# Attention with beacon keys and a maxout projection: loads as FP32 with casts on chip, and transposes by DMA, in place of casting DMAs and transposes on TensorE

## The chip, the cores and the metric

The kernel runs on one core of a Trainium2 chip (trn2). The metric is the device time of one execution in microseconds (us), so less is better. A change counts as faster or slower when it is beyond 2%. Names of the engines in the profile: PE is TensorE (PEld its weight loads), DVE is VectorE, ACT is ScalarE, POOL is GpSimd and SP is SyncE, which does nothing here but issue DMAs. A casting DMA changes the number type on the way. The DMA crossbar writes a tile transposed; such a transfer is called a turn below. PSUM is the memory that TensorE writes its products to.

## The reference

Eight batches, eight heads, 576 tokens and 16 beacon keys of head size 64. All inputs are FP32 in DRAM.

```python
B, H, S, Nb, D = 8, 8, 576, 16, 64
k_all = concat([beacon_k, k], axis=2); v_all = concat([beacon_v, v], axis=2)
scores = q @ k_all.T / sqrt(D)           # masked causally over k, beacons always visible
x = softmax(scores) @ v_all              # (B, H, S, D) -> (B*S, H*D) = (4608, 512)
h = max(x @ w1, x @ w2, x @ w3)          # w: (512, 768)
out = h @ w_out                          # w_out: (768, 512), out FP32 (4608, 512)
```

## The kernel before

Attention goes by batches, in each by four pairs of heads, in each by six chunks of scores. The projection, called FFN here, is cut into 22 units for every 512 tokens: 18 units of the first product (with the maximum taken on VectorE) and 4 of the second. They are put between the chunks of the next batch's attention, so that TensorE has work while ScalarE computes exponentials.

The loads of q, k, v and the weights are casting DMAs of GpSimd: FP32 is read and BF16 lands. Only the first two pairs come as FP32 by the SP and ACT queues and are cast on chip.

```python
def load_qk(b, hs):                      # the same form for v, w_in, w_out
    q_sb, k_sb, _ = load_tiles(b)        # BF16 tiles
    nc.gpsimd.dma_start(out=q_sb[:, hs, :], in_=q[b, hs].rearrange("h (p r) d -> p h (r d)", r=QR))
    # ... k and beacon_k
```

TensorE turns every pair (12 transposes for q, 16 for k), and VectorE copies the result out of PSUM. `qz` holds each head with zeros in the other head's 64 partitions.

```python
def emit_transposes(p):
    # ...
    q_ps = turn(qs, QP, QR)              # nc.tensor.transpose, 12 times
    k_ps = turn(ks, KP, KR)              # 16 times
    for e in range(2):
        hs = slice(64 * e, 64 * e + 64)
        nc.vector.tensor_copy(qz[p % NQZ][e][hs], q_ps[hs])
    nc.vector.tensor_copy(kT, k_ps.rearrange("d r p -> d p r"))
```

Masks of batches 0 and 1 are products on VectorE, because GpSimd is busy writing descriptors then. Later masks are selects on GpSimd. The output leaves through three buffers and the SP queue:

```python
y = ffn_y.tile([128, d_model], FP32, name="y")      # ffn_y has bufs=3
nc.vector.tensor_copy(y, ps)
nc.sync.dma_start(out[row : ...], y[...])
```

Emission order at the start: q and k of batch 0, v of batch 0, q and k of batch 1, first halves of the input weights, v of batch 1, second halves, w_out. In batch 1 nine FFN units are done, from batch 2 on 22 a batch.

The softmax here doesn't subtract the row's maximum and nothing guards it: scores larger than these inputs give would overflow.

## Time and profile before

| | before |
|---|---|
| median of runs | 336.8 us (336.05 to 337.81) |
| profiled span | 333.6 us |
| TensorE busy | 312.4 us, 94% |
| batch 2 begins (its first score product) | 59.9 us, 9 FFN units done |
| one batch after that | 35.4 us |

By stretches: the columns are the stretch, its length, busy us and instruction counts of each engine, granted TensorE clock, DMA share and GB/s.

```profile
core 0: us, PE busy (x) PEld busy (x) DVE busy (x) ACT busy (x) POOL busy (x), PEclk, DMA share, GB/s
0.00:20.00 20.00, 11.10 (x148) 6.31 (x152) 11.79 (x31) 11.44 (x30) 15.95 (x31) 1.00 1.23 167
...
40.00:60.00 20.00, 16.98 (x269) 9.95 (x268) 13.23 (x35) 13.27 (x40) 7.76 (x10) 1.00 1.27 149
60.00:80.00 20.00, 19.87 (x297) 11.27 (x295) 10.93 (x19) 12.99 (x37) 11.48 (x31) 1.00 0.48 73
...
120.00:320.00 200.00, 199.48 (x2392) 107.37 (x2387) 113.82 (x192) 106.24 (x285) 80.30 (x238) 1.00 0.41 63
```

From 120 to 320 us TensorE is busy 199.48 of 200 us (and 19.87 of 20 at 60 to 80), so only work taken off TensorE can shorten that part. The first 60 us have gaps.

What a pair's transposes cost there, from the timeline of TensorE (start, length, operation):

```profile
162.25 0.31 PE L247 MATMUL sc<-qz_109,kT 128*128 128x336 bf16 x1
162.49 0.45 PE L212 MATMUL sc<-ident,q_sb 96*64 96x96 bf16 x12
...
163.14 1.04 PE L334 MATMUL fps<-xT,w_sb 128*128 128x512 bf16 x4
```

From the start of the transposes at 162.49 us to the next projection matmul at 163.14 us is 0.65 us a pair.

### The profile page before, as it was taken

The page shows a single profiled execution, that of the slowest core. Times are in us where ns is not written, and L with a number is a line of the kernel's source. Part 1 is how long each engine was busy: PE and PEld are TensorE (multiplying, and loading weights), DVE is VectorE, ACT ScalarE, POOL GpSimd, SP SyncE. Part 2 cuts the span into 40 slices and gives each one's busy share as a digit, 9 for nine tenths or more (in the row PEclk, how much of TensorE's full clock was granted, in tenths as well). Part 3 has the DMA queues.
Part 4 walks back from the last instruction along what each step waited for, and adds up shares of the span by engine and source line. Part 5 has one row for each costly group of instructions (what it writes and reads, how often), then busy time and mean ns, then how long its engine had stood idle before and what let it go on. Part 6 is the DMA issues. An engine that isn't in the chain of part 4 may idle for free.

```text
span 333.6 us, 9819 instructions
## 1 busy us (share of the span) xinstructions
PE 312.4 (94%) x4064; PEld 171.4 (51%) x4064; DVE 190.4 (57%) x360; ACT 185.1 (55%) x505; POOL 153.4 (46%) x399
## 2 busy tenths in 40 slices
PE   1888788999999999999999999999999999999994
PEld 1454455555555555655565656555555554444441
DVE  4665467654655655656565565546556545555552
ACT  2798675765675557665765567656755562120210
POOL 8929851266545745474626654665433330000000
PEclk9998999999999999999999999999999999999998
DMA  8999999059702983099408940596002200402204
GB/s 172 151 177 127 165 161 154 9 71 178 98 2 29 175 120 28 2 162 160 26 4 116 194 36 4 78 182 88 2 2 65 66 0 2 127 2 63 62 2 126
DMA packets 62352, 28.24 MB, mean 85 GB/s; under 512 B 42980, under 2 KB 57404, under 8 KB 62308
## 3 DMA queue, kind: packets, MB, share of 16 engines
q0 software_dynamic: 55808, 16.98, 48.0%
q1 hardware_dynamic: 6188, 10.05, 10.5%
q10 hardware_dynamic: 312, 0.59, 0.7%
q8 instruction: 32, 0.52, 0.6%
q14 instruction: 12, 0.10, 0.1%
HBM read 35.13 MB, written 9.44 MB: 134 GB/s over the span
## 4 chain that ended last, share of the span: by engine, by line
PE 81%; DVE 8%; ACT 6%; DMA 2%; issue 1%; SPq 0%; DVEq 0%
PE fps L334 34%; PE fps L351 12%; PE sc L247 12%; PE pv L295 11%; PE sc L334 5%; ACT at_sb L255 5%; PE sc L212 3%; PE sc L351 2%; DMA q_120<-in_q_dram 2%; DVE kT L226 2%; DVE xT L312 2%; DVE hT L344 1%; DVE qz_109 L225 1%; PE fps L212 1%; ACT hT L342 0%
## 5 line engine op out<-in xcount | busy, mean ns | idle before, releaser
L255 ACT ACTIVATE at_sb<-sc 128x288 bf16<-128x288 f32 (+4 forms) x384 | 129.7, 404 | 64.3 <-PE sc L247 61.6
L334 PE MATMUL fps<-xT,w_sb 128*128 128x512 bf16 x564 | 144.2, 380 | 0.8
L273 POOL TENSOR_SCALAR_AFFINE_SELECT at_sb<-at_sb 128x132 bf16<-128x132 bf16 (+2 forms) x288 | 80.9, 300 | 102.6 <-ACT at_sb L255 97.6
L344 DVE TENSOR_TENSOR hT<-hT,fps 128x512 bf16<-128x512 bf16 x94 | 64.4, 686 | 58.1 <-PE fps L334 43.8
L334 PEld LDWEIGHTS <-w_sb 128*128 128x128 bf16 x648 | 59.0, 98 | 56.9 <-issue 2.5
L247 PEld LDWEIGHTS <-kT 128*128 128x128 bf16 (+1 forms) x384 | 37.2, 102 | 44.1 <-issue 4.6
L342 ACT CAST hT<-fps 128x512 bf16<-128x512 f32 x47 | 27.5, 585 | 48.2 <-PE fps L334 45.7
L351 PE MATMUL fps<-w_out_sb,hT 128*128 128x512 bf16 x180 | 44.1, 380 | 0.0
L312 DVE TENSOR_TENSOR xT<-pv,recip 128x288 bf16<-128x288 f32 x64 | 27.7, 454 | 26.1 <-ACT recip L307 19.8
L165 POOL DMA_DIRECT2D v_sb<-in_v_dram x40 | 34.2, 863 | 6.8 <-DMA w_out_sb<-in_moe_w_out_dram 3.7
L295 PE MATMUL pv<-at_sb,v_sb 128*32 128x288 bf16 (+4 forms) x1280 | 32.6, 240 | 0.8 <-DVE xT L312 0.8
L295 PEld LDWEIGHTS <-v_sb 128*32 128x32 bf16 (+1 forms) x1280 | 25.6, 97 | 13.3 <-issue 12.0
L359 DVE COPY y<-fps 128x512 f32<-128x512 f32 x30 | 20.7, 691 | 19.5 <-PE fps L351 16.5
L351 PEld LDWEIGHTS <-hT 128*128 128x128 bf16 x216 | 19.9, 98 | 22.4 <-DVE hT L344 3.1
L247 PE MATMUL sc<-qz_103,kT 128*128 128x288 bf16 (+2 forms) x96 | 28.0, 296 | 2.4 <-DVE kT L226 2.0
L247 PE MATMUL sc<-qz_107,kT 128*128 128x288 bf16 (+2 forms) x96 | 27.0, 283 | 2.2 <-DVE kT L226 1.3
L247 PE MATMUL sc<-qz_105,kT 128*128 128x288 bf16 (+2 forms) x96 | 27.8, 294 | 0.3 <-ACT at_sb L255 0.2
L247 PE MATMUL sc<-qz_109,kT 128*128 128x288 bf16 (+2 forms) x96 | 26.9, 282 | 1.0 <-DVE kT L226 0.6
L226 DVE COPY kT<-sc 128x592 bf16<-128x592 bf16 x28 | 21.7, 774 | 0.9
L334 PE MATMUL sc<-xT,w_sb 128*128 128x512 bf16 x84 | 21.6, 379 | 0.0
L269 DVE TENSOR_TENSOR at_sb<-at_sb,mask 128x264 bf16<-128x264 bf16 (+2 forms) x48 | 11.6, 264 | 15.5 <-ACT at_sb L255 15.2
L212 PEld LDWEIGHTS <-q_sb 96*64 96x64 bf16 x384 | 10.7, 112 | 14.0 <-DVE q_sb L152 7.5
(46 smaller groups left out, 205.5 us busy)
## 6 DMA issues: line engine op xcount, KB each, us to landing
out_dram<-y SPq DMA_DIRECT2D x24, 192.0 KB, 2.9
q_sb<-in_q_dram POOLq DMA_DIRECT2D x7, 576.0 KB, 6.2
k_sb<-in_k_dram POOLq DMA_DIRECT2D x7, 576.0 KB, 9.1
v_sb<-in_v_dram POOLq DMA_DIRECT2D x24, 128.0 KB, 5.2
out_dram<-y SPq DMA_DIRECT2D x24, 128.0 KB, 3.0
w_sb<-in_moe_w_dram POOLq DMA_DIRECT2D x24, 96.0 KB, 4.3
out_dram<-y SPq DMA_DIRECT2D x24, 64.0 KB, 2.8
v_sb<-in_v_dram POOLq DMA_DIRECT2D x8, 112.0 KB, 4.9
```

What stands on the lines that cost most here:

```text
L165: nc.gpsimd.dma_start(out=v_sb[lo : lo + n, t], in_=v[b, :, t0 : t0 + n, :].rearrange("h p d -> p h d"),)
L212: nc.tensor.transpose(ps[64 * e : 64 * e + 64, r, :], src[e][:, r * D : (r + 1) * D], ident[0:n, 0:n],)
L226: nc.vector.tensor_copy(kT, k_ps.rearrange("d r p -> d p r"))
L247: nc.tensor.matmul(ps[0:n, 0 : nr * w].rearrange("k (r p) -> k r p", p=w), kT[:, 128 * t : 128 * t + n], qz[p % NQZ][e][:, r0:r1, p0:QP], ...
L255: nc.scalar.activation(out=at_sb[0:n, t, j0 + e, r0:r1, p0:QP], in_=sc[e][0:n, 0 : nr * w].rearrange("k (r p) -> k r p", p=w), func=AF.Exp ...
L273: nc.gpsimd.affine_select(out=view, in_=view, compare_op=ALU.is_ge, fill=0.0, base=QR * p0 + r0 - k_tok[t], pattern=[[1, nr], [QR, p1 - p0 ...
L295: nc.tensor.matmul(ps[32 * j : 32 * j + 32, :, p0:QP], lhsT, at_sb[0:n, t, j, rs, p0:QP], start=(t == 0), stop=(t == n_kt - 1), tile_posit ...
L312: nc.vector.tensor_mul(xs.rearrange("c (r p) -> c r p", p=QP), ps, state["recip", hf])
L334: nc.tensor.matmul(ps, w_in[i][:, ct, 128 * ft : 128 * (ft + 1)], xT[:, ct, t0 : t0 + TOKB], start=(ct == 0), stop=(ct == n_ct - 1),)
L342: nc.scalar.copy(hT[:, ft, :], ps)
L344: nc.vector.tensor_max(hT[:, ft, :], hT[:, ft, :], ps)
L351: nc.tensor.matmul(ps, hT[:, ft, 128 * tt : 128 * (tt + 1)], w_out_sb[:, ft, :], start=(ft == 0), stop=(ft == n_ft - 1),)
```

## The change

The intent: take the transposes of batches 2 to 7 off the engine that limits the kernel, and free GpSimd from writing descriptors. Every load becomes a plain FP32 DMA of the SP queue into one of six staging tiles. Casts are done on VectorE, ScalarE or GpSimd. From batch 2 on the DMA crossbar turns q and k. `x` becomes a ring of four batches to make room, masks are all done on GpSimd, and batch 1 carries 18 FFN units in place of 9.

```diff
-        nc.gpsimd.dma_start(
-            out=q_sb[:, hs, :], in_=q[b, hs].rearrange("h (p r) d -> p h (r d)", r=QR)
-        )
+    st_pool = ctx.enter_context(tc.tile_pool(name="st", bufs=6))
+    def load_w(i, half):
+        st = new_stage(("w", i, half))               # FP32 staging tile
+        # ...
+            nc.sync.dma_start(out=dst[32 * j : 32 * j + 32], in_=wv[j, :, :, half * FH : (half + 1) * FH])
+    def cast_w(i, half, cast):                       # the same form for pairs, k, q, v, w_out
+        st = stage.pop(("w", i, half))
+        cast(w_in[i][:, :, half * FH : (half + 1) * FH], st[:, 0 : n_ct * FH].rearrange(...))
+    def turn_k(b, g):
+        nc.sync.dma_start_transpose(out=batch_tiles(b)[1][:, g]..., in_=k_src[:, g]...)
+    def turn_q(b, g):
+        nc.sync.dma_start_transpose(out=batch_tiles(b)[0][:, g]..., in_=q_src[:, g]...)
-        if b < 2:                                    # masks on VectorE
-            nc.vector.tensor_mul(view, view, m.to_broadcast([n, 2, nr, p1 - p0]))
-            return
+    at_step(0, 1, C(cast_pair, 2, by_pool, by_pool))
+    at_step(1, 1, C(cast_pair, 3, by_pool, by_pool))
+    at_step(1, 3, C(cast_w, 0, 0, by_dve))           # after pair 1, chunk 3
+    at_step(1, 5, C(cast_w, 1, 0, by_dve))
+    at_step(2, 1, C(cast_w, 2, 0, by_dve))
+    at_step(2, 2, C(cast_pair, 4, by_dve, by_pool))
+    # ...
+    at_step(3, 5, L(nc.gpsimd.memset, q_src, 0.0), L(nc.gpsimd.memset, k_src[...], 0.0))
+    for b in range(3, B):
+        p = (b - 1) * PPB
+        d = 1 if b == 3 else 0
+        at_step(p + d, 3, C(cast_k, b, 1, by_pool), L(turn_k, b, 0), L(turn_k, b, 1))
+        at_step(p + d, 4, C(cast_q, b, 0, by_pool), L(turn_q, b, 0))
+        at_step(p + 2, 2, C(cast_q, b, 1, by_pool), L(turn_q, b, 1))
+        # ... casts of v
```

(Cut: the tile shapes, among them a score tile that is packed without gaps, the plan's other steps, the ring's index.) `C` runs a cast, gives the staging tile back and issues the next loads, so the SP queue gets loads, turns and stores in the order in which the program reaches them.

## The prediction

> **What bounds it now.** The table of busy times by stretches shows TensorE busy for all 20 us of every 20 us from 60 to 320 us at full clock; before that it is busy 11.1, 16.3 and 17.0 of 20. The chain of waits puts 81% of the span on TensorE. VectorE (57%), ScalarE (55%) and GpSimd (46%) have room. In the timeline a batch takes about 35.4 us (kT copies at 58.2, 93.2 and 128.5 us).
>
> **What is removed.** In batches 2 to 7 the 28 TensorE transposes of each of 24 pairs go. In the timeline at 162.49 us they hold TensorE until 163.14, 0.65 us by starts, plus about 0.1 us that the change of operation costs where they follow a score product. 24 x 0.65 to 0.75 = 15.6 to 18 us, all on the critical path after 60 us. With them go VectorE copies of 0.46 + 0.46 + 0.77 us per pair (not critical) and two of four score buffers per pair. GpSimd loses some 75 us of descriptor writing; VectorE the mask products of batches 0 and 1 (11.6 us).
>
> **What is added.** GpSimd casts: from its two mask sizes (264 ns for 57 elements, 330 for 132) I estimate 0.21 us + 0.88 ns per element, so 0.67 us for 512, 0.9 for 768, some 11 us a batch beside 13.5 us of masks, in a period of 33: fits, but a pair with casts needs about 9.6 us in a pair of 8.2, caught up in the next. Crossbar turns move 1.8 MB a batch; the Trainium skill (Advanced Engine Details and Errata, section X-Bar Transpose) says they run about as fast as ordinary DMA, 350 to 400 GB/s (estimate: 5 us a batch; no run yet shows it). The sync queue takes turns, loads and stores in order, with waits on casts; of a batch's four output tiles only the fourth needs a store (the first's), which is issued ahead of the turns. The ring splits 18 FFN units into 256-column halves: about nothing.
>
> **Start.** Loads of FP32 read the same bytes; the first pair should land a little earlier (score at 8.7 us now). But GpSimd then has masks plus 2 us casts plus v casts in batch 0, and casts on VectorE wait in order for loads; I expect the first value product some 3 to 5 us later than 19.8 us, and batch 1 stretched by loads, to about 66 us instead of 59.9. Against that, batch 1 carries 18 FFN units instead of 9, 0.86 us of TensorE each, so 7.8 us less for the tail. Net about 0, give or take 5.
>
> **Sum.** 336.2 - 16.5 + 1.3 = 321 us; range 311 to 333. Chances: faster by over 2% 0.82, within 2% 0.12, slower 0.06.
>
> **What would show it right.** TensorE still busy 20 of 20 from about 70 us; a batch period of 32.6 to 33; transposes only in 8 pairs; VectorE busy down by about 40 us; GpSimd's idle time mostly waits on the exponential; batch 2 beginning at 62 to 70 us with 18 units done.
>
> **What would make it wrong.** The sync queue needing over 33 us a batch for turns (they then arrive late: score products waiting for a DMA); GpSimd casts near twice my estimate (value products waiting for masks); a start that loses more than 10 us to loads queued behind casts; or FFN units stalled by weights cast late.

## More of the kernel before

Bytes "landed" are the bytes that a DMA wrote.

The page of the profile of the kernel before: engine rows in tenths of each of 40 slices of 8.3 us, GB/s landed in each slice, the DMA queues with packets, MB and their time, and the chain that ended last by engine.

```profile
PE   1888788999999999999999999999999999999994
...
DMA  8999999059702983099408940596002200402204
GB/s 172 151 177 127 165 161 154 9 71 178 98 2 29 175 120 28 2 162 160 26 4 116 194 36 4 78 182 88 2 2 65 66 0 2 127 2 63 62 2 126
...
q0 software_dynamic: 55808, 16.98, 48.0%
q1 hardware_dynamic: 6188, 10.05, 10.5%
...
PE 81%; DVE 8%; ACT 6%; DMA 2%; issue 1%; SPq 0%; DVEq 0%
```

From the eighth slice on TensorE is busy without a gap. The DMA row is 8 and then 9 for the first seven slices (to 58 us, with 9.3 MB landed in the first 60 us at a mean of 155 GB/s) and then has pauses. GB/s counts the bytes that land, so for a casting load the bytes read are twice that (the page gives 35.13 MB read, of which the casting queue landed 16.98 MB). TensorE is 81% of the chain.

## The result, and the profile after

The changed kernel ran at 355.99 us (354.31 to 357.76, four runs) beside 336.8 us for the kernel before, ratio 1.057 (95% 1.051 to 1.063). It is slower by 5.7%. A ratio here and below is the mean time of one kernel's fast runs over that of the other's from the same rounds, so it is not quite the ratio of the medians that are quoted.

The page of the changed kernel, the same rows as before (slices of 8.9 us):

```profile
PE   2954655969965799999999999999999999999994
...
DMA  7999999999999999999999999996631300300304
GB/s 192 203 187 202 179 204 173 201 273 150 213 206 253 196 209 219 219 203 189 193 220 195 185 183 239 228 199 140 126 68 31 91 2 0 100 22 20 100 0 120
...
q1 hardware_dynamic: 129200, 55.59, 82.0%
...
PE 67%; DMA 20%; SPq 5%; DVE 3%; POOL 2%; issue 2%; ACT 1%; DVEq 0%; POOLq 0%
```

The DMA row is now 9 from the second slice to the 27th, about 240 us. The one queue that is left carries loads, turns and stores, and the time of its packets is 82.0% of the span. The bytes read are the same in both kernels (35.13 MB on both pages). The chain has 20% DMA, where it had 2%. TensorE has gaps up to the fourteenth slice.

By stretches, as before:

```profile
0.00:20.00 20.00, 11.53 (x110) 6.34 (x110) 8.31 (x16) 11.45 (x29) 9.96 (x30) 1.00 0.98 191
20.00:40.00 20.00, 12.48 (x196) 7.53 (x197) 8.14 (x14) 7.83 (x23) 8.04 (x22) 1.00 1.03 201
40.00:60.00 20.00, 10.11 (x143) 5.19 (x144) 10.14 (x12) 5.72 (x16) 16.07 (x28) 0.58 1.01 179
...
80.00:100.00 20.00, 19.23 (x267) 11.32 (x271) 11.71 (x21) 12.78 (x37) 10.87 (x31) 1.00 1.19 187
100.00:120.00 20.00, 12.06 (x69) 5.53 (x68) 3.69 (x6) 7.65 (x23) 8.71 (x26) 0.83 1.04 223
120.00:320.00 200.00, 195.42 (x2324) 113.99 (x2357) 88.56 (x148) 127.23 (x346) 116.11 (x350) 0.99 0.79 149
```

At 40 to 60 us TensorE is busy for 10.11 of 20 us (16.98 before) at a granted clock of 0.58, and again for only 12.06 at 100 to 120 us. The low clock appears only in stretches where TensorE is partly idle, but not in all of them: at 20 to 40 us it was busy for 12.48 us at 1.00. In the steady part it was 0.99.

Following the batches by the first score product and by the first output tile of each 512 tokens:

| | before | after |
|---|---|---|
| batch 2 begins | 59.9 us, 9 units done | 91.5 us, 18 units done |
| batch 2 (first output tile to the next group's first) | 35.4 us | 45.1 us |
| four batches after that | 141.5 us | 131.1 us |

The first score product of batch 2, before and then after, from the timelines of TensorE:

```profile
59.88 0.29 PE L247 MATMUL sc<-qz_103,kT 128*128 128x288 bf16 x1
```

```profile
91.50 0.65 PE L330 MATMUL sc<-qz,kT 128*128 128x288 bf16 x4
```

A first-product unit takes 0.86 us of TensorE, so nine units more are worth 7.8 us. The start therefore lost 31.6 - 7.8 = 23.8 us, batch 2 lost another 9.7, and the next four batches gave back 10.4, 2.6 us each. That makes 23.1 us; the last batch and the tail gained the rest, down to the 20.9 us between the two profiled spans. **The steady part did what was predicted. The start, and with it batch 2, did not.**

The chain of work up to the beginning of batch 2, by line: first the kernel before to 60 us, then the changed one to 92 us.

```profile
by line: ACT at_sb L255 29.6%; DMA q_120<-in_q_dram 12.4%; PE sc L247 9.6%; PE pv L295 8.9%; PE fps L334 7.8%; PE fps L212 4.1%; DVE kT L226 3.9%; issue 2.9%; ACT hT L342 2.6%; DVE xT L312 2.6%; DVE qz_105 L225 2.3%; DVE qz_103 L225 2.1%; D
```

```profile
by line: DMA st<-in_moe_w_dram 35.8%; DMA st<-in_k_dram 17.0%; DMA st<-in_q_dram 9.9%; PE fps L415 7.5%; SPq L203 6.2%; DMA st<-in_v_dram 5.5%; issue 2.3%; PE sc L330 2.3%; DVE hT L425 2.1%; DVE qz L176 1.8%; DVE xT L392 1.5%; SPq L260 1.2%
```

Before, the chain runs through exponentials (29.6%) and one early load. After, loads of weights, k, q and v are 68% of it. So in the start TensorE waits, by way of other engines, for DMAs. (The chain of this window ends with the SP queue issuing a load, not with batch 2's first product; it leaves TensorE's line of work at 87.3 us.) Its TensorE pieces lie from 62 us on, where a unit took 0.86 us as before, so the low clock of 40 to 60 us isn't on this chain.

Who did the waiting, from the list of waits of the changed kernel (total, times, longest):

```profile
DVE w_sb L280 <- DMA st<-in_moe_w_dram: 20.4, 5, 9.3
...
POOL k_562 L152 <- DMA st<-in_beacon_k_dram: 8.4, 1, 8.4
...
PE fps L415 <- DVE y L440: 6.4, 1, 6.4
```

VectorE waits for weights 20.4 us in all. GpSimd waits 8.4 us for one k. Masks on GpSimd, and copies and maxima on VectorE, stand behind these casts. The last line belongs to batch 2. The timeline of all engines shows it (SPq is the SP queue issuing):

```profile
101.03 1.17 SPq L237 DMA_DIRECT2D st<-in_q_dram  x2
...
102.29 1.04 SPq L448 DMA_DIRECT2D out_dram<-y  x2
...
104.12 7.47 SPq L203 DMA_DIRECT2D st<-in_v_dram  x5
...
109.67 0.69 DVE L440 COPY y<-fps 128x512 f32<-128x512 f32 x1 [9.33 <-DMA out_dram<-y]
```

The fourth output tile needs the first one's buffer. Its store was issued only at 102.29 us, after a batch's k and q loads, though the first tile was ready at 95.2; then its transfer landed among queued loads. VectorE waited 9.33 us, TensorE 6.44.

### The profile page after: what moved, and what is told of

Same layout as the page of the kernel before. It is cut to its first block, busy times and chain, and to the rows that moved or that the text cites. A ratio compares the mean times of both kernels' runs of the same rounds, so it can differ in the third digit from the quotient of the medians.

```text
span 354.5 us, 8835 instructions
## 1 busy us (share of the span) xinstructions
PE 306.2 (86%) x3421; PEld 171.7 (48%) x3464; DVE 157.9 (45%) x259; ACT 187.3 (53%) x505; POOL 182.0 (51%) x520
## 2 busy tenths in 40 slices
DMA packets 129242, 56.16 MB, mean 158 GB/s; under 512 B 113424, under 2 KB 122640, under 8 KB 129200
## 3 DMA queue, kind: packets, MB, share of 16 engines
q1 hardware_dynamic: 129200, 55.59, 82.0%
HBM read 35.13 MB, written 9.44 MB: 126 GB/s over the span
## 4 chain that ended last, share of the span: by engine, by line
PE 67%; DMA 20%; SPq 5%; DVE 3%; POOL 2%; issue 2%; ACT 1%; DVEq 0%; POOLq 0%
PE fps L415 32%; PE fps L432 10%; PE sc L330 10%; DMA st<-in_moe_w_dram 9%; PE pv L373 9%; DMA st<-in_k_dram 4%; PE sc L415 4%; SPq L203 4%; DMA st<-in_q_dram 3%; DMA out_dram<-y 2%; PE sc L432 1%; DMA st<-in_v_dram 1%; POOL k_src L232 1%; POOL at_sb L350 1%; DVE hT L425 1%
## 5 line engine op out<-in xcount | busy, mean ns | idle before, releaser
L338 ACT ACTIVATE at_sb<-sc 128x288 bf16<-128x288 f32 (+4 forms) x384 | 131.1, 404 | 71.9 <-PE sc L330 70.5
L350 POOL TENSOR_SCALAR_AFFINE_SELECT at_sb<-at_sb 128x132 bf16<-128x132 bf16 (+2 forms) x384 | 110.0, 305 | 99.7 <-ACT at_sb L338 93.8
L415 PE MATMUL fps<-xT,w_sb 128*128 128x512 bf16 (+1 forms) x626 | 145.9, 358 | 12.1 <-DVE y L440 6.4
L415 PEld LDWEIGHTS <-w_sb 128*128 128x128 bf16 x720 | 67.6, 98 | 63.4 <-issue 13.5
L330 PE MATMUL sc<-qz,kT 128*128 128x288 bf16 (+4 forms) x384 | 81.6, 302 | 5.3 <-DVE kT L177 3.7
L440 DVE COPY y<-fps 128x512 f32<-128x512 f32 x32 | 22.1, 692 | 32.3 <-PE fps L432 14.6
L373 PEld LDWEIGHTS <-v_sb 128*32 128x32 bf16 (+1 forms) x1280 | 27.3, 101 | 15.8 <-issue 13.2
L373 PE MATMUL pv<-at_sb,ones 128*32 128x288 bf16 (+4 forms) x640 | 22.3, 253 | 14.3 <-DVE xT L392 9.1
L385 ACT ACTIVATE lnd<-pv 128x288 f32<-128x288 f32 x32 | 13.5, 422 | 25.5 <-PE pv L373 24.9
L373 PEld LDWEIGHTS <-ones 128*32 128x32 bf16 (+1 forms) x640 | 15.5, 101 | 21.7 <-issue 20.4
L218 POOL CAST v_sb<-st 128x512 bf16<-128x512 f32 (+1 forms) x40 | 23.4, 614 | 2.4 <-DMA st<-in_v_dram 2.4
L232 POOL CAST k_src<-st 128x256 bf16<-128x256 f32 (+1 forms) x60 | 21.3, 399 | 0.8 <-DMA st<-in_k_dram 0.8
L280 DVE CAST w_sb<-st 128x1536 bf16<-128x1536 f32 x6 | 8.9, 1486 | 20.4 <-DMA st<-in_moe_w_dram 20.4
L248 POOL CAST q_src<-st 96x768 bf16<-96x768 f32 x20 | 15.9, 821 | 0.0
(70 smaller groups left out, 95.2 us busy)
```

The source lines that it names most:

```text
L218: cast(v_sb[0:n, t].rearrange("p h d -> p (h d)"), st[0:n, i * H * D : (i + 1) * H * D],)
L232: cast(k_src[0:n, g, :, t], src[:, g])
L330: nc.tensor.matmul(ps[0:n, 0 : nr * w].rearrange("k (r p) -> k r p", p=w), kT[:, g, j0 // 2, 128 * t : 128 * t + n], qz[:, g, j0 + e, r0:r ...
L338: nc.scalar.activation(out=at_view(at_sb, t, j0 + e, r0, r1), in_=sc[e][0:n, 0 : nr * w], func=AF.Exp, scale=scale,)
L350: nc.gpsimd.affine_select(out=view, in_=view, compare_op=ALU.is_ge, fill=0.0, base=QR * p0 + r0 - k_tok[t], pattern=[[1, nr], [QR, p_max[t ...
L373: nc.tensor.matmul(ps[32 * j : 32 * j + 32, :, p_min[t] : QP], lhsT, at_view(at_sb, t, j, hf * RH, (hf + 1) * RH).rearrange("k (r p) -> k ...
```

## The experiments

Two theories were stated after this reading. RATE: FP32 lands too slowly; what batch 2 needs is 17.7 MB landed (197 GB/s over 90 us; 1.8 MB of it are batch 2's own turns) in place of 9.3 MB. ORDER: engines and queues run in order, and what attention needs stands behind casts, loads and stores that are late. Each run below lists its edit against the changed kernel, unless it says otherwise. Against the kernel before, by the 2% rule, e_hybrid2 is the same and e_half, e_half_w, e_half_mask, e_mask and e_all are unclear; what is read from these is their difference from the changed kernel.

### Kinds of loads by themselves (m_rates)

No attention, wrong output. Each kind of load is issued alone, and VectorE notes the landing.

```diff
+ for kind, dt, issue in [("pair", FP32, by_sp), ("pair", BF16, by_pool), ("w", FP32, by_sp), ...]:
+     for d in phase(kind, dt, issue): landed(d)
```

> A measurement, wrong output on purpose: each kind of load alone, one after the other, FP32 by the sync queue, cast to BF16 by the GpSimd queue, and FP32 (no cast) by the GpSimd queue. Theory RATE (the FP32 loads land too slowly): per byte read, FP32 by the sync queue takes about 1.5 times as long as the cast load (about 195 against 310 GB/s read, from the two traces). If the bytes written are what counts, FP32 by the GpSimd queue is as slow as by the sync queue; if the hardware queue itself is slow, it is as fast as the cast load. Rival ORDER (the rates are alike, and only the order of waits of casts costs): the times of FP32 and cast loads are within 15% of each other. Two queues in turn (sync and ScalarE) should change nothing if the 16 engines are the limit. The four crossbar turns of a batch alone should take 12 to 14 us.

| first issue to last landing, us | FP32 by SP | cast by GpSimd | FP32 by GpSimd |
|---|---|---|---|
| four pairs of q, k | 12.4 | 11.3 | 14.9 |
| three weight halves | 12.4 | 9.9 | 12.7 |
| v of two batches | 13.5 | 12.2 | 14.5 |
| w_out | 6.6 | 7.4 | not run |

The landing of the second and third weight half, FP32 by SP and then cast, from VectorE's timeline:

```profile
50.53 0.15 DVE L102 COPY sink<-f 128x1 f32<-128x1 f32 x1 [3.33 <-DMA f<-in_moe_w_dram]
53.81 0.15 DVE L102 COPY sink<-f 128x1 f32<-128x1 f32 x1 [3.13 <-DMA f<-in_moe_w_dram]
...
62.32 0.15 DVE L102 CAST sink<-b 128x1 f32<-128x1 bf16 x1 [2.32 <-DMA b<-in_moe_w_dram]
64.50 0.15 DVE L102 CAST sink<-b 128x1 f32<-128x1 bf16 x1 [2.03 <-DMA b<-in_moe_w_dram]
```

Apart from the first latency a third (0.79 MB of FP32) lands every 3.4 us on average as FP32 and every 2.3 us when it is cast on the way: 1.45 times as long, near the 1.5 of RATE. The whole phases took 1.25 (weights), 1.10 (q, k) and 1.11 times as long (v), so for q, k and v ORDER's "within 15%" held. Issued by GpSimd both times, the cast load was faster for all three kinds, so the size that lands matters; it came nowhere near half of the time for half of the bytes. And w_out went the other way. As FP32 it landed at 328 GB/s (149.0 to 153.5 us), the input weights at 234 (43 to 52 us). So it is not FP32 as such that lands at about 200 GB/s; the form of a load counts too (w_out: 800 packets for 1.57 MB, all 128 partitions in one DMA; input weights: 1728 packets for 2.36 MB, 32 partitions in one). No run changed the form of the loads in the kernel.

The Trainium skill (DMA: Bandwidth & Descriptors, section Issuing engine by pattern) says that the hardware path is generally faster than GpSimd's. For the same FP32 loads this agrees (12.4, 12.4 and 13.5 us by SP, 14.9, 12.7 and 14.5 by GpSimd), but a load that GpSimd's queue cast on the way ended sooner than either for three of the four kinds. The same page, section Issuing engines are not separate DMA queues, says that DMAs from several engines share the same 16 DMA engines; this agrees: SP and ACT in turn took 12.75 us for the weights, and 13.3 for v.

A batch's four crossbar turns alone, their issue and VectorE's note of the last landing, from the timeline of all engines:

```profile
184.14 2.94 SPq L206 DMA_TRANSPOSE kT<-k_src  x2
187.13 6.15 SPq L213 DMA_TRANSPOSE qz<-q_src  x2
...
195.21 0.15 DVE L218 CAST sink<-qz 128x1 f32<-128x1 bf16 x1 [2.81 <-DMA qz<-q_src]
```

That is 11 us for 1.84 MB, 167 GB/s overall, against 5 us estimated in the prediction.

### Transposes back on TensorE (e_no_xbar)

```diff
-    N_PE = 2
+    N_PE = 8          # all pairs loaded and turned as in batches 0 and 1
```

> The changed kernel, but q and k of all batches loaded per pair, cast and turned on TensorE (no crossbar, no key-major loads). If the crossbar gives 2.6 us a batch as the traces say (period 35.4 to 32.8), the period goes back to about 35.4 us, and from that alone the time rises by 13 to 16 us over the changed kernel. Theory RATE says that batch 2 then needs fewer small packets and no turns, so its stalls (some 12 us against the later period) go: about 360 us in all. Rival ORDER leaves the start as it is and gives about 370 us.

363.8 us, ratio 1.078 (1.071 to 1.085). The start is the same (first output tile at 93.7 against 94.5 us), and the period after batch 2 is 36.0 to 36.3 us against 32.3 to 33.1. The crossbar is worth some 3.3 us a batch against this variant. It is not what lost the start. Batch 2 took 36.8 us here against 45.1, so 8.3 us of its loss go when turns and loads by key go together; which of the two it is, this run doesn't separate. The total lies between the two forecasts.

### Five output buffers (e_ybufs)

```diff
-    ffn_y = ctx.enter_context(tc.tile_pool(name="ffn_y", bufs=3))
+    ffn_y = ctx.enter_context(tc.tile_pool(name="ffn_y", bufs=5))
```

> The changed kernel with five output buffers in place of three: the copy of the fourth output tile of batch 2 no longer waits 9.3 us for a store that stands behind loads in the sync queue. If that wait is a cost of its own: 7 to 9 us less (about 348 us). If DMA sets the pace there anyway (theory RATE), the time comes back as a wait for the turned k and q of batch 3: 0 to 4 us less.

351.5 us, ratio 1.043 (1.038 to 1.047): 4.5 us less than the changed kernel. The wait for the store is gone, but batch 2 still takes 42.0 us. In its chain the turn of batch 3's q is now a piece of 7.0 us: with the stores out of the way, TensorE waits for the late turn (3.6 us idle).

### The start of the kernel before with crossbar turns from batch 3 on (e_hybrid)

```diff
-    N_PE = 2
+    N_PE = 3
-    loads = [L(load_pair, 0), ..., L(load_w, i, 0), ...]     # FP32, batches 0 to 2, weights
+    load_qk_first(0); load_qk_first(1); load_qk(0, ...); load_v(0, t); ...   # casting DMAs, as before
+    if b < 2: nc.vector.tensor_mul(...)                      # masks as before
     # q, k of batches 3 to 7: FP32 by SP in four staging tiles; v by casting DMA
```

> The start of the kernel before (batches 0 to 2, all weights and all v by casting loads on the GpSimd queue, mask products on VectorE in batches 0 and 1, q and k of batches 0 to 2 turned on TensorE) with the crossbar for batches 3 to 7 alone, whose q and k come as FP32 by the sync queue and are cast on GpSimd. Theory RATE (only the start costs, the crossbar is worth 2.6 us a batch): 336.8 - 5 x 2.6 = 324 us, with batch 2 beginning at about 60 us. If instead the crossbar or the casts cost in the later batches: 333 to 340 us.

354.1 us, ratio 1.052 (1.048 to 1.056). This missed the 324 us. The waits of VectorE, and of the SP queue, show why:

```profile
DVE y L465 <- DMA out_dram<-y: 30.7, 4, 12.7
```

```profile
SPq L223 <- POOL k_src L259: 39.7, 3, 14.5
```

VectorE waited 30.7 us for output stores in four batches (TensorE 17.3 of it). The SP queue itself stood 39.7 us before loads, waiting for k casts on GpSimd, and stores stood behind. (The expectation of e_hybrid2 below calls the 30.7 us a wait of TensorE; it is the wait of VectorE.)

### Weights by casting DMA (e_w_pool), and another order (e_order)

```diff
 # e_w_pool; the same for w_out, issued at three steps of the plan
-            nc.sync.dma_start(out=dst[32 * j : 32 * j + 32], ...)
+            nc.gpsimd.dma_start(out=w_in[i][32 * j : 32 * j + 32, :, half * FH : (half + 1) * FH], ...)
 # e_order: the same loads; q, k of batch 1 ahead of the weights, weight casts moved into batch 1,
 # the FFN units of batch 1 begun two chunks later
-    loads += [L(load_pair, 3)] + [L(load_w, i, 0) for i in range(3)]
-    loads += [L(load_pair, p) for p in range(PPB, 2 * PPB)] + [L(load_w, i, 1) for i in range(3)]
+    loads += [L(load_pair, 3)] + [L(load_pair, p) for p in range(PPB, 2 * PPB)]
+    loads += [L(load_w, i, 0) for i in range(3)] + [L(load_v, 1, 0), L(load_v, 1, 1)]
+    loads += [L(load_w, i, 1) for i in range(3)]
```

> The changed kernel, with its weights landed as BF16 by casting DMAs of GpSimd (no staging tile, no VectorE cast for them); q, k, v, turns, ring and masks as in the changed kernel. In the run of load kinds the two sets of three weight halves and w_out took 12.4 + 12.4 + 6.6 us of DMA time as FP32 and 9.9 + 9.9 + 7.4 us cast, and VectorE no longer waits in order for them (20.4 us of its waits). Theory RATE (the start is held by the rate at which FP32 lands): about 10 us faster than the changed kernel, ratio to the kernel before about 1.025, first y copy near 84 to 88 us. Theory ORDER (the start is held by casts and stores that stand in order behind late loads, weights above all): 10 to 20 us faster, about 1.00 to 1.025. Both agree in direction; no change would refute both for the weights, and leave q, k, v loads.

> The changed kernel with the same loads and bytes, all by the SP queue, in another order: q and k of batch 1 before the first weight halves, v of batch 1 before the second halves, casts of weights moved into batch 1, batch 2's k and q after them. Theory RATE: the same bytes must land before batch 2 can start, so within 3 us of the changed kernel, ratio about 1.05. Theory ORDER: attention of batches 0 and 1 no longer stands behind weight casts; 10 to 20 us faster, ratio 1.00 to 1.03.

e_w_pool ran at 351.9 us, ratio 1.046 (1.039 to 1.052), and e_order at 353.9 us, ratio 1.049 (1.045 to 1.054). Neither gave the 10 us. In e_w_pool TensorE waited 15.7 us in one place for a q cast on GpSimd that stood behind weight descriptors, so the line had only moved: the first output tile came at 98.5 us, later than in the changed kernel (94.5) and than the 84 to 88 expected, while batch 2 fell to 36.7 us. In e_order the first output tile came 6.3 us earlier (88.2 against 94.5), and batch 2 gave it back: TensorE waited 10.2 us for a store's buffer. Read as a verdict between RATE and ORDER, e_order's small gain looked like RATE, but because of the store it is a weak one.

### The hybrid mended (e_hybrid2, e_hybrid3)

```diff
 # e_hybrid2 against e_hybrid
-    ffn_y = ctx.enter_context(tc.tile_pool(name="ffn_y", bufs=3))
+    ffn_y = ctx.enter_context(tc.tile_pool(name="ffn_y", bufs=6))
-        at_step(p + d, 2, C(cast_k, b, 0, by_pool))
+        at_step(p + d, 2, C(cast_k, b, 0, by_dve))
-    at_step(7, 0, L(nc.gpsimd.memset, q_src, 0.0), ...)
+    at_step(2, 2, L(nc.vector.memset, q_src[:, 0], 0.0))     # and the other half a pair later
 # e_hybrid3 against e_hybrid2
-at_pool.tile([128, 4, at_off[n_kt]], BF16)                   # heads outside, key tiles packed inside
+at_pool.tile([128, 4 * at_off[n_kt]], BF16)                  # key tiles outside, heads inside
-        clear_qz(0); clear_qz(1)                             # eight clears ahead of the first cast
+    clear_qz(0, (0, 1))                                      # two ahead, the others during batch 0
 # and the k casts of a piece are split in two steps
```

> The first hybrid (start of the kernel before with casting DMAs of GpSimd and VectorE masks for batches 0 and 1, crossbar turns for batches 3 to 7 only, their q and k as FP32 by SP, v by casting DMA) with its three faults mended: six y buffers instead of three, k casts of the steady batches on VectorE instead of GpSimd, and all clearing at the start or in batch 0 on VectorE. If the 30.7 us that the first hybrid's TensorE waited on y stores were the whole loss, it lands at 320 to 327 us, ratio 0.95 to 0.975. If the crossbar itself or its traffic holds the steady batches, it stays above 0.985, with periods over 34 us and waits on q or k turns in the chain.

> The second hybrid lost 9.4 us to the kernel before by the first output tile (86.0 against 76.6 us), then gained 2.6 to 2.9 us a batch. Its records name two causes: VectorE clears 8 slices before the first cast (7.2 us against 5.5), and exponentials wait for VectorE masks 10.0 us in 11 places (1.2 us in one place before), because in the packed score tile the mask of two heads spans columns of later chunks. Here the score tile is laid out by key tile, as in the kernel before, the clearing is spread over batch 0, and the k casts of a piece are split in two. If these are the causes: first output tile at 77 to 79 us, total 321 to 325 us, ratio 0.955 to 0.968. If the first tile stays over 83 us, the loss of the start is of another kind.

e_hybrid2: 331.5 us, ratio 0.984 (0.980 to 0.989), with no wait for stores over 0.6 us. It missed the 320 to 327: the first output tile came at 86.0 against 76.6 us. Its list of waits named the cause, here beside the same line of the kernel before:

```profile
ACT at_sb L356 <- DVE at_sb L370: 10.0, 11, 2.0
```

```profile
ACT at_sb L255 <- DVE at_sb L269: 1.2, 1, 1.2
```

The mask covers two heads in one operation. In the packed tile of the changed kernel its range spans columns of later chunks, so the next exponentials waited for it, 10.0 us in eleven places. e_hybrid3 changed the layout, the clears and the k casts together: the wait is gone from its list, and it ran at 323.2 us, ratio 0.965 (0.959 to 0.970). It is correct and beats both kernels. The total is as expected, but the first tile came at 82.6 us (81.15 in the repeat below) and not at 77 to 79, so 4.6 to 6 us of the start's loss are not explained.

### Half of the bytes (e_half, e_half_w)

This keeps every engine's work and its order and takes bytes away. Packets go with them (90891 in place of 129242), and half of the reading too, so it shows what the loads' duration costs, not which property of a load makes it long. Wrong output.

```diff
-                in_=src[b, :, t0 : t0 + n, :].rearrange("h p d -> p h d")
+                in_=src[b, 0:HH, t0 : t0 + n, :].rearrange("h p d -> p h d")     # HH = H // 2
-                st[0:n, i * H * D : (i + 1) * H * D],
+                twice(st[0:n, i * H * D : i * H * D + HH * D]),   # the cast reads the half twice
 # the same for pairs, q, k and input weights; e_half_w: for the input weights alone
```

> The changed kernel with half of every q, k, v and input weight load left out (wrong output on purpose): half of the heads, or of the weight rows, is loaded and each cast reads that half twice, so all casts, turns, masks, matmuls, waits and their order stay. Sorting the records: the changed kernel landed 17.7 MB in its first 90 us and batch 2 began at about 91 us, the kernel before 9.3 MB in 60 us. Theory RATE (what batch 2 waits for is bytes landed at about 195 GB/s): about 9 MB fewer, batch 2 begins near 60 us, batch 2 itself loses its 10 us, total 315 to 328 us, ratio 0.935 to 0.975. Theory ORDER (what counts is that stores, casts and loads stand in line behind one another): the line is as long, so at most 10 us gained, ratio over 1.02.

> The same for the input weights alone (wrong output on purpose): 2.36 MB of FP32 fewer. At the 190 GB/s that the weights landed with in the changed kernel, theory RATE expects 10 to 13 us off the start, 342 to 346 us, ratio about 1.02. If weights are not what the start waits for, under 4 us. Theory ORDER: the weight casts of VectorE still wait in order for their loads, but these end sooner; it expects up to the 20.4 us of those waits if they are the cause.

e_half ran at 329.0 us, ratio 0.979 (0.974 to 0.984), 27 us below the changed kernel. ORDER had said over 1.02, so ORDER alone fails. RATE's range of 315 to 328 was just missed. Batch 2 began at 74.35 us (91.5 before), not near 60, and then took 36.7 us. The chain up to 74 us, by line:

```profile
by line: PE fps L426 15.7%; POOL at_sb L361 14.7%; PE pv L384 12.0%; DMA st<-in_k_dram 11.6%; PE sc L341 8.5%; ACT at_sb L349 5.8%; POOL k_src L238 5.5%; issue 4.4%; PE sc L170 3.6%; DMA st<-in_moe_w_dram 2.7%; POOL k L157 2.7%; SPq L140 2.
```

Loads of k are down to 11.6% and those of weights to 2.7%; GpSimd masks, at 14.7%, now come ahead of them. Of the 33.5 us that start and batch 2 had lost, 17.2 came back in the start and 8.4 in batch 2. e_half_w ran at 344.4 us, ratio 1.024 (1.020 to 1.029), 11 us less, as RATE had it; ORDER allowed that too. One of its four executions took 1039 us, and the profile fell on it, so only its times of the other three are used.

### Masks of batches 0 and 1 back on VectorE (e_mask, e_half_mask), with controls (e_after2, e_layout, e_mask2)

```diff
+        if b < 2:
+            nc.vector.tensor_mul(view, view, m.to_broadcast([n, 2, nr, wm]))   # as in the kernel before
+            return
 # with the score tile laid out by key tile; e_layout: the layout alone; e_after2: the changed kernel
```

> The half-byte kernel (wrong output on purpose) with the masks of batches 0 and 1 as VectorE products, as in the kernel before, instead of GpSimd selects (score tile laid out by key tile so that no mask covers columns of later chunks). With half of the bytes the changed kernel's order still ran 8 us over the predicted 321 us, with GpSimd busy 10.0 of 10 us at 10 to 20 and at 30 to 40 us. Theory GPSIMD-START (what is left of the loss is masks and casts sharing GpSimd in batches 0 and 1): 4 to 8 us off, 321 to 325 us, ratio 0.955 to 0.97. If within 2 us of 329, what is left is something else (order of waits, clock).

> The changed kernel with all of its loads, and the same masks moved to VectorE. Theory RATE (bytes bound the start): relieving GpSimd changes nothing, 352 to 358 us, ratio 1.045 to 1.063. Theory GPSIMD (masks and casts sharing GpSimd are what stretched the start): 8 us or more faster, under 348 us.

> The changed kernel unaltered, on the chip of the next two runs. If the 11 us between it and the run with VectorE masks was a difference of chips, it lands near 345 us here or the VectorE-mask kernel near 355; if not, 353 to 357 us, ratio 1.05 to 1.06.

> The changed kernel with only the score tile laid out by key tile (masks stay on GpSimd). Selects are per head, so no mask covers columns of other chunks in either layout: within 2 us of the changed kernel if the gain of the VectorE-mask run was the masks' engine; 8 us or more faster if it was the layout.

> The run with VectorE masks again, unaltered: 343 to 346 us, ratio 1.02 to 1.03, if it was no difference of chips, and the same DMA time for the queue of loads (255 us summed over the span, against 284 to 291 in the runs with GpSimd masks).

| | us | ratio (95%) |
|---|---|---|
| e_half_mask | 331.4 | 0.984 (0.977 to 0.992) |
| e_mask | 344.7 | 1.025 (1.018 to 1.032) |
| e_after2 | 355.7 | 1.057 (1.053 to 1.061) |
| e_layout | 356.9 | 1.061 (1.057 to 1.066) |
| e_mask2 | 346.0 | 1.031 (1.024 to 1.038) |

The last three ran on one chip. So the 10 us of e_mask is no difference of chips and not the layout: it is the masks' engine. RATE had expected nothing here and was wrong on that. Together with e_half this says that the two act on the same waits: the loads are late, and in the changed kernel masks stand on GpSimd behind casts that wait for them (8.4 us behind one k). Taking away either the lateness or what stands behind it helps. That is a reading of the two results and of the list of waits; no run isolates it. At half the bytes the masks' move gained nothing, but that run ran into something else, shown by the timeline of all engines:

```profile
31.84 5.21 POOL L523 MEMSET q_src<- 96x6144 bf16 x1
32.03 5.44 DVE L156 CAST q<-st 96x768 bf16<-96x768 f32 x1
...
39.58 0.66 PE L360 MATMUL sc<-qz,kT 128*128 128x288 bf16 x2 [7.73 <-DVE kT L182]
```

While GpSimd clears `q_src` (5.21 us), a VectorE cast of this shape that takes 0.49 to 0.65 us in the changed kernel takes 5.44, and TensorE waits 7.73 us. The Trainium skill (SBUF — State Buffer, section Who interferes with whom) says that VectorE in its two-port modes and GpSimd exclude each other for a whole instruction. This agrees, though the trace doesn't show in which mode the cast ran; in the changed kernel the same clear stretched a weight cast to 3.97 us from 0.96. So e_half_mask doesn't tell whether masks on GpSimd were what was left at half the bytes.

### Does GpSimd work slow the transfers? (m_gpsimd)

In e_mask the first six loads, issued without any wait, landed faster too: on one chip, the k of pair 3, the last of them, was cast, after a wait for its landing, at 20.9 us in e_mask2 against 23.3 in e_after2. Over the whole span the packets of the SP queue took 253 us there (74.0% of 341.5) and 287 us in e_after2 (80.9% of 354.6), for the same 55.59 MB.

```diff
+ whats = ["none", "pool_mask", "pool_cast", "dve_mask", "dve_cast", "act_exp", "none"]
+ for kind, what in [("w", x) for x in whats] + ...:
+     got = phase(kind, FP32, by_sp); end = work(what); ...     # both end before the next begins
```

> No attention and no projection (wrong output on purpose): three FP32 weight halves, then four FP32 pairs, then v of two batches, by the SP queue, each set again and again with one engine working beside it for as long: nothing; GpSimd mask selects (128x132); GpSimd casts (128x512 FP32 to BF16); VectorE mask products; VectorE casts; ScalarE exponentials; nothing again. Alone they took 12.4, 12.4 and 13.5 us. Theory A (GpSimd work slows landing): 14 to 15.5 us beside GpSimd selects or casts, within 0.5 us of the idle figure beside VectorE and ScalarE work. Theory B (the rates in the kernel follow the mix of loads): all within 0.5 us of the idle figure.

Stretches inside the weight phases, beside GpSimd selects, GpSimd casts, VectorE products, and nothing:

```profile
core 0: us, DVE busy (x) ACT busy (x) POOL busy (x), PEclk, DMA share, GB/s
16.00:27.00 11.00, 0.31 (x2) 0.00 (x0) 9.09 (x29) 1.00 1.05 212
33.00:44.00 11.00, 0.31 (x2) 0.00 (x0) 9.98 (x17) 1.00 1.00 210
48.50:60.00 11.50, 9.98 (x45) 0.00 (x0) 0.00 (x0) 1.00 0.98 205
...
109.00:120.00 11.00, 0.31 (x2) 0.00 (x0) 0.00 (x0) 1.00 1.04 211
```

Weights landed at 212, 210, 205 and 211 GB/s, and in 13.2 to 13.4 us beside selects, casts, exponentials or nothing. For weights theory A, that GpSimd work slows landing, falls. The other loads, by the same timeline: q and k ended 14.5 us after the phase began with nothing beside, 13.8 beside selects and 14.0 beside casts; v 14.1, 14.2 and 14.8. Only v beside casts was slower, by 0.7 us, which is over theory B's 0.5 but far from the 2.4 us between e_mask2 and e_after2. This agrees with the Trainium skill (SBUF — State Buffer, section SBUF: two separate sides), which says that engine ports and DMA ports don't contend. Why the same six loads landed sooner in e_mask, and why its queue took less time for the same bytes, stays open.

### All the small remedies at once, and the hybrid again (e_all, e_hybrid3b)

```diff
 # e_all: e_order + masks of batches 0 and 1 on VectorE + ffn_y bufs=5; all loads FP32 by SP
 # e_hybrid3b: e_hybrid3 unaltered, same chip
```

> The changed kernel with the three remedies at once that leave its loads alone: VectorE masks in batches 0 and 1 (10 us by themselves), the other order of loads and casts (2 us) and five y buffers (4.5 us). If order of waits is all, they add up or more: 338 us or below, ratio under 1.005. If bytes landed bound the start (17.1 MB of FP32 before batch 2, about 80 us at 217 GB/s, against 57 in the kernel before), 340 us or more, and less than the sum is gained.

> The third hybrid again: 322 to 326 us, ratio 0.955 to 0.97, and, whatever the run above shows, at least 12 us below it if casting on the way is what keeps the start short.

e_all: 342.6 us (339.7 to 343.2; a fourth execution, at 348.4 us, was slow), ratio 1.013 (1.003 to 1.023). That is only 2 to 3 us below the mask runs by medians (4 to 6 by ratios), and not the 338 of adding up. But it doesn't settle the matter: the clear of `q_src` ran into a q cast here too (5.35 us), and TensorE waited 7.91 us for what stood behind it. No run moved the clear alone. Batch 2 took 43.7 us in it, and at its end TensorE waited for a crossbar turn:

```profile
123.02 0.93 PE L349 MATMUL sc<-qz,kT 128*128 128x288 bf16 x4 [5.14 <-DMA qz<-q_src]
```

e_hybrid3b: 324.1 us, ratio 0.961 (0.953 to 0.969), 18 us below e_all on the same chip. Its page:

```profile
PE   1896878899999999999999999999999999999993
...
PE 81%; DVE 7%; ACT 5%; DMA 3%; issue 2%; SPq 0%; DVEq 0%; ACTq 0%
```

TensorE is 81% of the chain, as in the kernel before. Batch 2 begins at 63.9 us (nine units done, as in the kernel before), and the first output tiles of successive groups are 32.2 to 32.8 us apart, against 35.4. By the sixth group it is 10.5 us ahead (243.0 against 253.5). It differs from e_all in more than how its early loads land: it also turns batch 2 on TensorE and casts v on the way in the steady part. So the 18 us are the price of the all-FP32 start as it stands, clear included, not of one cause.

## Why the prediction was wrong

- **Right: what the crossbar saves.** Predicted period 32.6 to 33 us; measured 32.3 to 33.1 after batch 2, from 35.4. TensorE's transposes were on the critical path.
- **Right: the price of casts on GpSimd.** Estimated 0.67 and 0.9 us; measured 0.61 and 0.82 us. GpSimd holds in the steady part, where TensorE was busy 195.42 of 200 us.
- **Near: VectorE.** It lost 32.5 us of busy time (190.4 to 157.9), not about 40.
- **Mis-sized: the turns.** 5 us a batch was estimated from the Trainium skill (350 to 400 GB/s); measured 11 us alone. In the steady part that stayed hidden. In batch 2, where loads still queue, it did not: TensorE waits 3.6 us (e_ybufs) and 5.1 us (e_all) for a turn of q.
- **Wrong, and the main step: "Start. Loads of FP32 read the same bytes ... Net about 0, give or take 5."** The step that failed is to take equal reading for equal time. The bytes read are the same, but 17.7 MB landed before batch 2 in place of 9.3, and the rate rose only from 155 to 197 GB/s. A third of the input weights lands in 3.4 us as FP32 and 2.3 us when cast. Batch 2 began at 91.5 us, not 62 to 70: 23.8 us net of its nine extra units. Halving the bytes at the same order of work took 27 us off in all. The DMA row before, 8 and then 9 from the start, had shown little room for longer loads; the prediction read TensorE's gaps in that part and not this row. That the loads' duration is the main cost is shown; that landed bytes, and not the form of the loads, set it is argued.
- **Left out: loads ahead of the store.** "... only the fourth needs a store (the first's), which is issued ahead of the turns" held even in batch 2, but there the store stood behind a batch's k and q loads and cost TensorE 6.4 us; five buffers gave 4.5 us back.
- **The listed danger was close, but turned about.** A start that loses more than 10 us "to loads queued behind casts" was named as what could make it wrong. It was mostly casts, and attention behind them, queued behind loads. Moving masks of two batches off GpSimd gave 10 us. The clear of `q_src` on GpSimd (5.21 us), which no term of the prediction counts, fell into the same stretch.

The terms don't add up to one sum, since they sit on the same waits: 27 us by bytes, 10 by masks, 4.5 by buffers, 2 by order, 13 by the last three together. What stays open: which limit holds these FP32 loads at about 200 GB/s when w_out landed at 328, why the loads took less time with the masks on VectorE, and what holds the last 4.6 to 6 us at the start of the hybrid.

## What to carry to other kernels

Cost a load by the bytes that land and by the rate at which a load of the same form landed in a profile, not by the bytes read; if the DMA row is full in a stretch, expect a change that doubles the landed bytes there to lengthen it (here 1.1 to 1.25 times for three kinds of loads by themselves, and shorter for a fourth). A gain in the steady part can be kept without that price: leave the start as it is, and change over once the DMA row has room, which here gave 0.96 in place of 1.06. In a queue that runs in order, ask of each late item what stands behind it: stores behind loads, masks behind casts, casts behind a clear on the engine that shares a port.

## What the Trainium skill lacked or had wrong

- DMA: Bandwidth & Descriptors, Issuing engine by pattern: "HWDGE (sync/scalar) is generally faster" held for the same FP32 loads, but it says nothing of data that is wanted as BF16: the same three weight halves took 12.4 us as FP32 by SP and 9.9 us cast by GpSimd, w_out 6.6 and 7.4. No page gives the cost of a casting load beside a plain one.
- Advanced Engine Details and Errata, X-Bar Transpose (TRN2): 350 to 400 GB/s expected. Four turns of 1.84 MB in all took 11 us alone, 167 GB/s, and most slices of the time on the way showed 190 to 225 GB/s.
- SBUF — State Buffer, Who interferes with whom: correct and useful, but it gives no size for the case met here: a GpSimd clear of 5.21 us stretched VectorE casts of 0.49 to 0.96 us to 3.97, 4.40, 5.35 and 5.44 us.
- No page has it: plain FP32 loads of 192 to 576 KB, one after the other in the SP queue, landed at 179 to 201 GB/s in the three 20 us stretches of the first 60 us of the changed kernel and at 205 to 234 by themselves, w_out (768 KB a load) at 328. The page (DMA: Bandwidth & Descriptors, section Bandwidth) gives 341 GB/s for a single load of 1 MB issued from GpSimd and no figure for streams of FP32 loads like these.
